# mLSTM cell and gated MLP on one core: the second chunk's queries change their queue, and their block transposes their place

## The chip, the cores and the metric

The kernel runs on one core of a Trainium2 chip. The metric is the device time of one execution in microseconds (us); a lower one is better. Times are given as the median of several runs. One execution was also profiled, and the views of the profile that are quoted here all come from it; their times count from the start of its span. The engines are PE (TensorE, with PEld its weight loads), DVE (VectorE), ACT (ScalarE), POOL (GpSimd) and SP (SyncE, which here only issues transfers). A name with q behind it, such as SPq, is the engine's sequencer, which issues transfers and waits.

## The reference

Two blocks follow each other. The first is an mLSTM cell over 768 time steps for 4 batches of 8 heads of 40 elements; the second is a dense layer, a quick GELU and another dense layer over the 3072 tokens.

```python
for t in range(S):                                   # S = 768
    m_new = np.maximum(f_gate[:, :, t] + m, i_gate[:, :, t])
    f_stab, i_stab = np.exp(f_gate[:, :, t] + m - m_new), np.exp(i_gate[:, :, t] - m_new)
    C = f_stab * C + i_stab * outer(v_t, k_t)        # 40 x 40 for each batch and head
    n = f_stab * n + i_stab * k_t
    y[:, :, t] = sigmoid(o_gate_t) * (C @ q_t) / max(|n . q_t|, 1)
x = y as (3072 tokens, 320)
h = x @ w_in                                         # 320 x 2048
out = (h * sigmoid(1.702 * h)) @ w_out               # 2048 x 320
```

## The kernel before

Time is cut into six chunks of 128 steps (`w` = 0 to 5), and the recurrence within a chunk becomes products of matrices: scores of keys and queries (`scores`, tile `p_s`), weighted by exponentials of the gates (`weights`, tile `wt`), times the values (`values`, tiles `p_o` and `p_i`), with a state that is carried from chunk to chunk (`carry`, tile `p_c`, which multiplies the keys by the values scaled by the gates, `vw`, and whose result DVE adds to the state in L611 and L579). For each chunk, the outputs of four batches are transposed into `xT` (512 tokens), go through the first product (`up` for chunk 0, `up_fast` later; tile `p_h`, then the GELU, L641) and the second product (`down`, later `down_fast`; tile `p_out`).

The order of all work is written out by hand: the program is issued in the order of the Python calls, each engine runs its own instructions in that order, and waits are put in where one instruction needs another's result. The main loop runs over the chunks. In chunk `w` the first product is cut into eight steps `j`, and between them stands what prepares chunk `w + 1`: loads, gates, transposes. The second product is cut into blocks `i`, and a table (`attention`) says after which block each part of the next chunk's cell runs. For chunk 0 the second product has 16 blocks of four 128 x 320 products; `carry` of chunk 1 comes after block 3, `scores` after block 6, `values` after blocks 8 and 9.

The weights come into the kernel as pairs of 32-bit words and are turned into fp32 on the chip. There are 20 pieces of 128 x 512; pieces 0 to 9 belong to `w_in` and pieces 10 to 19 to `w_out`. `fetch(n)` loads a piece through the sync queue (L167). `convert(n)` takes two ScalarE instructions (L243 and L247) and then four DVE instructions (L256, L257, L259, L265). These conversions run during the first product of chunk 0 (pieces 3 to 16) and in the second (17 before block 0, 18 before block 4, 19 before block 5).

For chunk 1 the queries are loaded by `load_squares` into the tile `q_sq`, by four transfers of 320 KB (L108). One quarter of the rows is written by each, so a reader needs all four. `block_transposes(1, n)` with n = 1, 3, 5, 7 then makes the transposed queries `qT` of batch n // 2, one DVE instruction each (L394), which `scores` and `values` read. The keys of chunk 1 are loaded by L120 and transposed on PE (`transposes`, L386, with ScalarE's copies L388).

In the sync queue the transfers of chunk 0's first product stand in this order: the keys of chunk 1 (L120, `t_sb`), pieces 10 to 12, the values of chunk 1 (L120, `v_st`), pieces 13 to 17, `spread` (L403: four transfers that spread the rows of the running maxima, `m_row`, over the partitions of `wt`), pieces 18 and 19, the output gates (L122, `eo`), and the gates of chunk 2 (L92). POOL issues the queries of chunk 1 behind `scale(0, 1)` (L588), and later the small rows of the gates (L304 to L352). After the transposes, `q_sq` serves as a buffer for the turned outputs (`seam_in`) and then takes the queries of chunk 2.

PSUM has two pools: `ps_m` with four tiles (`p_h`, `p_out` and others) and `ps_a` with two (`p_t`, `p_c`, `p_s`, `p_o`, `p_i`), so a product can only begin when a reader has freed the tile of an earlier one.

Of the kernel before, what the change touches and what calls it, by code (L numbers as in the profile page):

```python
# [26 lines left out]
def kernel(  # L27
# [12 lines left out]
    nc = tc.nc  # L40
    B, H, S, D = q.shape
    BH = B * H
# [27 lines left out]
    V, A, G, T = nc.vector, nc.scalar, nc.gpsimd, nc.tensor  # L70
# [28 lines left out]

        return k_of(w)[t, h, :] if w < 2 else k_st[t, h * D:h * D + DP]  # L100

    def load_squares(w, what, queue=nc.sync):
        for dst, src in [((k_sq, k), (q_sq, q))["kq".index(c)] for c in what]:
            x = src[:, :, w * L:(w + 1) * L, :].rearrange("b (p two) (r c) d -> two r (b p) (c d)", two=2, c=4)
            for i in range(2):
                for n in range(2):
                    r, at = slice(i * 64 + n * 32, i * 64 + n * 32 + 32), (1 - n) * 32
                    queue.dma_start(out=dst[r, at:at + BH // 2 * 4 * D].rearrange("r (j x) -> r j x", x=4 * D), in_=x[i])  # L108

    def load(w, what, bs=slice(0, B)):  # L110
        hs = slice(bs.start * H, bs.stop * H)
# [121 lines left out]
    def convert(n):  # L233
        convert_begin(n)
        convert_end(n)

    def convert_begin(n):
        convert_high(n)
        convert_low(n)
# [9 lines left out]
    def convert_end(n):  # L249
        convert_mid(n)  # L250
        convert_add(n)
# [88 lines left out]
    def masks():  # L340
        V.tensor_reduce(out=odd, in_=full.rearrange("p (j two) -> p two j", two=2)[:, 1], axis=AX.X, op=OP.add)
        V.memset(odd[BH:2 * BH, :], 0.0)
        V.tensor_scalar(out=even, in0=odd, scalar1=-1.0, scalar2=1.0, op0=OP.mult, op1=OP.add)
# [46 lines left out]
    def block_transposes(w, n):  # L390
        b, (to, name, src) = n // 2, ((kT, "kT", k_sq), (qT, "qT", q_sq))[n % 2]
        at, n = 32 + b * NP * 4 * D, NP * 4 * D
        to[w, b] = work.tile([128, NP, L], FP, tag=name, bufs=4, name=name)
        V.transpose(out=to[w, b].rearrange("d j (r c) -> d j c r", c=4),  # L394
                    in_=src[:, at:at + n].rearrange("r (j c d) -> r j c d", c=4, d=D)[:, :, :, 0:32])

    def spread(w):

        for c in range(2):
            x = wt[w, c] = work.tile([L, NJ, 2, HL], FP, tag="wt", bufs=2, name="wt")  # L400
            for n in range(2):
                src = m_row[w][n, c * PH:(c + 1) * PH].rearrange("h t -> (h t)")
                nc.sync.dma_start(out=x[n * HL:(n + 1) * HL].rearrange("s j i t -> s (j i t)"),  # L403
                                  in_=src.unsqueeze(0).to_broadcast([HL, PH * HL]))
# [177 lines left out]
    def scale(w, c, part=0, parts=1):  # L582
        n = PH // parts
        hs = slice(c * PH + part * n, c * PH + (part + 1) * n)
        if part == 0:
            vw[w, c] = work.tile([L, PH, D1], FP, tag="u", name="vw")
        e = cols[w][:, 2 * BH + hs.start:2 * BH + hs.stop].unsqueeze(2).to_broadcast([L, n, D1])
        G.tensor_tensor(out=vw[w, c][:, part * n:(part + 1) * n], in0=v_st[:, hs, :], in1=e, op=OP.mult)  # L588

    def wait_for(x):  # L590

        G.tensor_copy(out=mark, in_=x[:, 0:1])
# [21 lines left out]
    def up(w, j, between):  # L614


        x = xT[w].rearrange("p c b t -> p c (b t)")
        ph = {}

        def full(j, first, cs=range(2)):  # L620
            for c in cs:
                for i in range(2):
                    f = 2 * j + i
                    for n in range(2):
                        t = slice(n * W // 2, (n + 1) * W // 2)
                        T.matmul(ph[j][i][:, t], w_in_sb[:, c, f * 128:(f + 1) * 128], x[:, c, t],  # L626
                                 start=(first and c == 0 and n == 0), stop=(not first and c == 1 and n == 1))

        def rest(j, start, stop):
            n = 2 if j >= NF // 4 else 1  # L630
            for h in range(n):
                t = slice(h * W // n, (h + 1) * W // n)
                for i in range(2):
                    r = slice(i * 64, i * 64 + 64)
                    T.matmul(ph[j][i][:, t], w_in_x[r, j, :], x[r, 2, t], start=(start and h == 0),  # L635
                             stop=(stop and h == n - 1))

        def gelu(j):
            g = gs[w, j] = gp.tile([128, 2, W], FP, tag="g", name="g")
            for i in range(2):  # L640
                A.activation(out=g[:, i, :], in_=ph[j][i], func=AF.Gelu_apprx_sigmoid)  # L641

        def open_pair(j):
            ph[j] = [ps_m.tile([128, W], FP, tag="m", name="p_h") for _ in range(2)]

        open_pair(j)
        full(j, True, range(1 if j == 0 else 2))
        if j == 0:
            open_pair(1)
            full(1, True, range(1))  # L650
            full(0, True, range(1, 2))
        rest(j, False, True)
        gelu(j)
        between()
        if j:
            open_pair(j + 1)
        rest(j + 1, j > 0, False)
        full(j + 1, False, range(1 if j == 0 else 0, 2))
        gelu(j + 1)
# [178 lines left out]
    def run(calls):  # L838
        for f, *args in calls:
            f(*args)  # L840
# [62 lines left out]
    for w in range(NW):  # L903
        more = w + 1 < NW
        if w == 0:
            for j in range(NF // 2):
                if j % 2 == 0:
                    ahead, behind = converted[j // 2]
                    run([(convert, p) for p in ahead] + [(fetch, p) for p in fetched.get(j // 2, ())])
                    up(w, j, lambda: run([(columns_turn, 1) if p is None else (convert, p) for p in behind]))  # L910
                if j == 6:
                    load(1, "o")
                if j == 1:
                    wait_for(w_in_sb[:, 1, 512:1024])
                    scale(0, 1)
                    load_squares(1, "q", G)
                    load(1, "v")
                if j < B and j % 2:
                    carry(0, j // 2)
                if j == 3:  # L920
                    masks()
                    gates(1)
                    columns_in(1)
                if j == 4:
                    spread(1)
                if j >= B:
                    transposes(1, j - B)
                if j in (4, 5):
                    block_transposes(1, 2 * j - 7)
        else:  # L930
            token_sums(w)
            if more:
                gates(w + 1)
                load(w + 1, "o")
            for j in range(NF // 2):
                up_fast(w, j)
                if w == 1 and j < 4:
                    weight_sums(j)
                if more and j == 2:
                    load(w + 1, "vk")  # L940
                    columns_in(w + 1)
                    spread(w + 1)
                if more and j:
                    for n in ((), (0, 2), (4,), (6, 1), (3,), (5, 7), ())[j - 1]:
                        block_transposes(w + 1, n)
                if more and j == 7:
                    columns_turn(w + 1)
                if 2 <= j < 6:
                    hidden_difference(w, j - 2)
                if j >= 6:  # L950
                    hidden_sums(w, (j - 6,), G)
            gelu_fast(w, NF // 2 - 1)
            hidden_sums(w, (2, 3), V)
        side = attention(w + 1) if more else {}
        if w == 0:
            block_transposes(1, 5)
            block_transposes(1, 7)

            blocks = [(lambda b=b, n=n: down(w, b, n)) for n0 in (0, 2) for b in range(B) for n in (n0, n0 + 1)]
        else:  # L960
            blocks = down_fast(w, 0) + down_fast(w, 1)
        for i, block in enumerate(blocks):
            if w == 0 and i in (0, 4, 5):
                convert((17, 18, 19)[max(i - 3, 0)])
            if w + 2 < NW and i == (6 if w == 0 else 0):
                load_gates(w + 2)
            if w + 2 < NW and i == 13:
                load_squares(w + 2, "kq" if w else "k")
            if w == 0 and i == 15:
                load_squares(w + 2, "q")  # L970
            block()
            run(side.get(i, []))
            if w == 0 and i in (11, 13):
                input_sums(slice(0, 4) if i == 11 else slice(4, 8))
# [30 lines left out]
```

## Time and profile before

| what | value |
| --- | --- |
| median of 3 runs | 468.26 us (466.65 to 468.61) |
| the profiled execution, its own time | 469.14 us |
| its span | 467.4 us |
| PE busy | 460.4 us (99%) |
| DVE, ACT, POOL busy | 341.7, 189.6, 165.2 us |
| first product of chunk 0, last step to second product's first block | PE idle until 67.71 us |
| second product of chunk 0 | 67.71 to 112.6 us |
| L108 for chunk 1's queries, issued by POOL | 36.93 to 39.70 us |
| L394 for chunk 1's queries | two from 62.36 us, two from 76.21 us |

A line of a timeline has the start, the time from the first start to the last end, the engine, the line of the kernel, the operation, the tile written and the tiles read, and how many instructions of the kind stand together; in brackets is the idle time before it with what ended it. A line of the chain of waits has the start, the length and what ran. In the DMA view a queue's line has packets, megabytes and the time that its packets took as a share of the 16 transfer engines: q1 is the sync queue's, q10 ScalarE's, q0 the one for transfers issued by POOL. Ends of PE's instructions are modelled, so differences of starts are used for PE.

### The profile page before, as it was taken

Reading aid. Unit: us, or ns where it says so; the run is one execution under the profiler, and the core shown is the slowest. Engines: PE = TensorE matmul, PEld = TensorE weight load, DVE = VectorE, ACT = ScalarE, POOL = GpSimd, SP = SyncE. Lnnn points to the kernel's source line nnn. Section 1 sums busy time; section 2 is a strip of 40 time slices with the busy share of each in tenths; the row PEclk is TensorE's granted clock in tenths of the full one; section 3 lists DMA queues with packets and bytes.
Section 4 is the critical chain, followed back from the end, with each engine's and each line's share of the span. In section 5 each row is a group of like instructions: output and inputs, shape, how many; then the busy total and the mean of one; then the engine's idle time right before and its main releaser. Section 6 shows DMA issues by size and latency. Waiting matters only on the chain.

```text
span 467.4 us, 12367 instructions
## 1 busy us (share of the span) xinstructions
PE 460.4 (99%) x5063; PEld 387.4 (83%) x5063; DVE 341.7 (73%) x698; ACT 189.6 (41%) x433; POOL 165.2 (35%) x157
## 2 busy tenths in 40 slices
PE   8999999999999999999999999999999999999997
PEld 6867876776778999678999778999878999876996
DVE  5788779989788976688875778877768866545612
ACT  5686369500536700554800453900444810254100
POOL 5103314300798700266800257610148510157100
PEclk9999999999999999999999999999999999999999
DMA  8999999028995034988124999114999405000000
GB/s 164 194 275 191 193 270 234 6 61 185 172 147 119 3 80 128 193 120 134 34 60 113 199 131 162 22 41 117 182 133 120 94 18 139 28 1 0 1 29 29
DMA packets 133833, 52.87 MB, mean 113 GB/s; under 512 B 101984, under 2 KB 129584, under 8 KB 133776
## 3 DMA queue, kind: packets, MB, share of 16 engines
q1 hardware_dynamic: 125024, 48.96, 54.3%
q0 software_dynamic: 704, 1.46, 2.0%
q10 hardware_dynamic: 8048, 1.66, 1.8%
q8 instruction: 40, 0.66, 0.6%
q14 instruction: 17, 0.14, 0.1%
HBM read 44.52 MB, written 7.54 MB: 111 GB/s over the span
## 4 chain that ended last, share of the span: by engine, by line
PE 92%; ACT 2%; POOL 1%; DMA 1%; issue 1%; SPq 1%; DVE 1%; POOLq 0%; ACTq 0%; DVEq 0%
PE p_out L818 33%; PE p_h L709 27%; PE p_h L717 8%; PE p_out L764 6%; PE p_h L626 5%; PE p_c L602 2%; PE p_o L503 2%; PE p_s L459 2%; PE p_i L511 2%; PE p_h L635 1%; DMA bits<-in_moe_w_out_dram 1%; PE p_t L386 1%; PE p_s L448 1%; SPq L120 1%; ACT w_out_sb L243 0%
## 5 line engine op out<-in xcount | busy, mean ns | idle before, releaser
L755 POOL TENSOR_TENSOR g<-g,parts 128x512 f32<-128x512 f32 x30 | 38.2, 1273 | 188.5 <-DVE parts L747 181.1
L743 ACT COPY parts<-p_h 128x256 f32<-128x256 f32 x40 | 14.9, 374 | 149.4 <-PE p_h L709 147.5
L818 PE MATMUL p_out<-w_out_sb,g 128*128 128x160 f32 x480 | 69.5, 301 | 0.0
L818 PEld LDWEIGHTS p_out<-w_out_sb,g 128*128 128x128 f32 x480 | 66.5, 190 | 0.9
L709 PE MATMUL p_h<-xT,w_in_sb 128*128 128x256 f32 x240 | 67.0, 388 | 0.0
L690 ACT ACTIVATE g<-g 128x512 f32<-128x512 f32 x80 | 50.1, 631 | 39.2 <-DVE g L750 24.6
L709 PEld LDWEIGHTS p_h<-xT,w_in_sb 128*128 128x128 f32 x240 | 43.8, 190 | 18.5 <-issue 6.7
L823 DVE TENSOR_TENSOR o_sb<-o_sb,p_out 128x160 f32<-128x160 f32 x70 | 21.4, 317 | 41.2 <-PE p_out L818 40.6
L818 PE MATMUL p_out<-t_sb,s 128*128 128x160 f32 x320 | 47.2, 300 | 0.0
L746 DVE TENSOR_TENSOR t_x<-p_h,parts 128x256 f32<-128x256 f32 x40 | 16.6, 415 | 39.0 <-PE p_h L717 34.5
L818 PEld LDWEIGHTS p_out<-t_sb,s 128*128 128x128 f32 x320 | 44.4, 190 | 0.2
L709 PE MATMUL p_h<-t_x,s_in 128*128 128x256 f32 x160 | 41.1, 379 | 0.0
L717 PE MATMUL p_h<-xT,w_in_x 64*128 64x512 f32 (+1 forms) x192 | 39.8, 540 | 0.0
L435 ACT ACTIVATE wt<-wt,cols 128x64 f32<-128x64 f32 x160 | 38.8, 333 | 0.1
L764 PE MATMUL p_out<-w_out_sb,g 128*128 128x320 f32 x128 | 36.1, 437 | 1.0 <-ACT g L641 0.7
L709 PEld LDWEIGHTS p_h<-t_x,s_in 128*128 128x128 f32 x160 | 30.4, 190 | 4.2
L764 PEld LDWEIGHTS p_out<-w_out_sb,g 128*128 128x128 f32 x128 | 23.9, 190 | 11.1 <-ACT g L641 0.9
L747 DVE TENSOR_TENSOR parts<-p_h,t_x 128x512 f32<-128x512 f32 x40 | 27.7, 692 | 3.6
L754 ACT COPY g<-p_h 128x512 f32<-128x512 f32 x30 | 17.4, 580 | 30.4 <-PE p_h L717 25.1
L626 PE MATMUL p_h<-xT,w_in_sb 128*128 128x256 f32 x128 | 29.7, 385 | 0.0
L717 PEld LDWEIGHTS p_h<-xT,w_in_x 64*128 64x128 f32 x192 | 16.9, 186 | 14.7 <-issue 13.5
L750 DVE TENSOR_TENSOR g<-p_h,parts 128x512 f32<-128x512 f32 x40 | 27.6, 691 | 1.4
(204 smaller groups left out, 842.7 us busy)
## 6 DMA issues: line engine op xcount, KB each, us to landing
wt<-m_row SPq DMA_DIRECT2D x20, 256.0 KB, 5.0
k_sq<-in_k_dram SPq DMA_DIRECT2D x16, 320.0 KB, 6.4
q_sq<-in_q_dram SPq DMA_DIRECT2D x16, 320.0 KB, 10.4
out_dram<-o_sb SPq DMA_DIRECT2D x24, 160.0 KB, 1.9
eo<-in_o_gate_dram SPq DMA_DIRECT2D x5, 640.0 KB, 8.4
bits<-in_moe_w_in_dram SPq DMA_DIRECT2D x6, 512.0 KB, 10.9
q_sq<-x_row SPq DMA_DIRECT2D x10, 256.0 KB, 2.9
v_st<-in_v_dram SPq DMA_DIRECT2D x14, 160.0 KB, 5.0
```

Of the source, the lines that this page charges most:

```text
L435: A.activation(out=x[:, h, :], in_=x[:, h, :], func=AF.Exp, scale=-1.0, bias=cols[w][:, c * PH + h:c * PH + h + 1])
L626: T.matmul(ph[j][i][:, t], w_in_sb[:, c, f * 128:(f + 1) * 128], x[:, c, t], start=(first and c == 0 and n == 0), stop=(not first and c == ...
L690: A.activation(out=gs[w, j][:, i, :], in_=gs[w, j][:, i, :], func=AF.Gelu_apprx_sigmoid)
L709: T.matmul(out, a, x[n], start=start, stop=stop)
L717: T.matmul(row[:, t], w_in_x[r, j, :], rest_x[r, 2, t], start=(not late and h == 0), stop=(late and h == n - 1))
L747: V.tensor_tensor(out=y[:, half_w:3 * half_w].rearrange("p (a t) -> p a t", a=2), in0=flat[:, half_w:3 * half_w].rearrange("p (a t) -> p a ...
L750: V.tensor_tensor(out=g[:, 1, :], in0=row1, in1=y[:, half_w:3 * half_w], op=OP.add)
L754: A.copy(out=g[:, 0, :], in_=row0)
L755: G.tensor_tensor(out=g0, in0=g0, in1=u, op=OP.add)
L764: T.matmul(po, gs[w, f // 2][:, f % 2, b * L:(b + 1) * L], w_out_sb[:, f, :], start=(f == 0), stop=(f == NF - 1))
L818: T.matmul(po, a(f), b[:, f, :], start=(f == 0), stop=(f == NH - 1))
L823: V.tensor_tensor(out=dst, in0=x, in1=po, op=OP.add)
```

## The change

The four loads of chunk 1's queries go from POOL, where they stood behind `scale(0, 1)` in step j = 1, to the sync queue, behind `spread(1)` in step j = 4. The parameter `queue` of `load_squares` goes. The four block transposes of the queries, of which two stood in steps j = 4 and 5 and two ahead of the conversion of piece 17, now stand together behind that conversion, at the beginning of block 0 of the second product. Nothing else moves: the instructions of PE and ScalarE are the same in the same order, DVE and POOL and SP differ in these places alone.

```diff
-    def load_squares(w, what, queue=nc.sync):
+    def load_squares(w, what):
...
-                    queue.dma_start(out=dst[r, at:at + BH // 2 * 4 * D].rearrange("r (j x) -> r j x", x=4 * D), in_=x[i])
+                    nc.sync.dma_start(out=dst[r, at:at + BH // 2 * 4 * D].rearrange("r (j x) -> r j x", x=4 * D), in_=x[i])
...
                 if j == 1:
                     wait_for(w_in_sb[:, 1, 512:1024])
                     scale(0, 1)
-                    load_squares(1, "q", G)
                     load(1, "v")
...
                 if j == 4:
                     spread(1)
+                    load_squares(1, "q")
                 if j >= B:
                     transposes(1, j - B)
-                if j in (4, 5):
-                    block_transposes(1, 2 * j - 7)
...
         if w == 0:
-            block_transposes(1, 5)
-            block_transposes(1, 7)
 
             blocks = [(lambda b=b, n=n: down(w, b, n)) for n0 in (0, 2) for b in range(B) for n in (n0, n0 + 1)]
...
             if w == 0 and i in (0, 4, 5):
                 convert((17, 18, 19)[max(i - 3, 0)])
+                if i == 0:
+                    for n in (1, 3, 5, 7):
+                        block_transposes(1, n)
```

## The prediction

> **What bounds the kernel now.** I read the page first, then the chain of waits and the timelines of the stretch that the change touches (about 27 to 115 us), then the DMA view of parts of it. Two lines of the page:
>
> ```profile
> PE 460.4 (99%) x5063; PEld 387.4 (83%) x5063; DVE 341.7 (73%) x698; ACT 189.6 (41%) x433; POOL 165.2 (35%) x157
> DMA  8999999028995034988124999114999405000000
> ```
>
> TensorE is busy for all but 7.0 us of 467.4, so an edit that moves no matmul can only win back waits of PE, or add some. The DMA row has 9s in slices 1 to 6, which are 11.7 us each: from 12 to 82 us the transfer engines are full, and there the order of transfers decides what comes late. The chain of waits leaves PE in one long stretch near the change (start, length, what):
>
> ```profile
> 57.12 2.33 SPq L120
> ...
> 60.67 5.14 DMA bits<-in_moe_w_out_dram
> ...
> 76.35 0.52 POOL vw L588
> ...
> 80.08 6.66 PE p_out L764 x24
> ```
>
> It runs through the sync queue (v's load, L120), the landing of an output weight piece, ScalarE's conversions and POOL's `vw`, back to PE. PE's timeline has the stalls:
>
> ```profile
> 49.85 2.00 PE L635 MATMUL p_h<-xT,w_in_x 64*128 64x256 f32 x16
> 55.34 1.04 PE L386 MATMUL p_t<-ident,t_sb 128*128 128x128 f32 x8
> 56.29 3.72 PE L626 MATMUL p_h<-xT,w_in_sb 128*128 128x256 f32 x16
> 59.94 2.54 PE L635 MATMUL p_h<-xT,w_in_x 64*128 64x256 f32 x16
> 65.97 1.04 PE L386 MATMUL p_t<-ident,t_sb 128*128 128x128 f32 x8
> 67.71 3.50 PE L764 MATMUL p_out<-w_out_sb,g 128*128 128x320 f32 x12 [0.71 <-ACT g L641]
> 71.49 5.65 PE L764 MATMUL p_out<-w_out_sb,g 128*128 128x320 f32 x20 [0.28 <-DVE w_out_sb L265]
> 77.69 2.40 PE L602 MATMUL p_c<-vw,t_sb 64*64 64x41 f32 x128 [0.55 <-POOL vw L588]
> ```
>
> From start to start, so that modelled ends play no part: (a) the 16 L635 take 2.47 us (59.94 to the next group at 62.41) where the same 16 took 1.93 at 49.85: 0.54 lost. (b) Eight L386 to the next group: 1.74 here, 0.95 at 55.34: 0.79. (c) Twelve L764 take 3.78; 48 of them later run from 99.56 to 112.58, 0.271 each, so 3.35 with 0.1 for the first: 0.43. (d) Twenty take 6.20 against 5.42 and two changes of kind at 0.1: 0.58. (e) The 128 L602 take 2.32 to 80.01; the same 128 take 2.01 at 154.40: 0.31. Together 2.65 us, say 2.7, of the 7.0 that PE idles. All five stand behind ScalarE, which runs in order, and ScalarE stands behind DMA:
>
> ```profile
> 54.50 0.67 ACT L243 ACTIVATE w_out_sb<-s_in 128x512 f32<-128x512 f32 x1 [6.61 <-DMA s_in<-in_moe_w_out_dram]
> 65.91 0.69 ACT L243 ACTIVATE w_out_sb<-bits 128x512 f32<-128x512 f32 x1 [3.66 <-DMA bits<-in_moe_w_out_dram]
> ```
>
> A conversion waits for its piece, and the GELUs that free PE's banks (L641) and the exponentials that `vw` needs wait behind it.
>
> **The change, part by part.** *POOL's four issues go.* They are 2.77 us on POOL (36.93 to 39.70); its next work is at 49.04 and waits for DVE, so the issues themselves are worth 0. What they set off is not. The DMA view of 39 to 48 us:
>
> ```profile
> q0 software_dynamic: 358, 1.23, 81.4%
> q1 hardware_dynamic: 1630, 0.26, 28.9%
> ```
>
> The second chunk's queries (4 x 320 KB, 1.31 MB), issued by POOL, take four fifths of all engines for 9 us while the sync queue, with k and output pieces 10 to 12 queued, moves 0.26 MB. It moved 2.52 MB in the 7 us from 63. So POOL's load passes the sync queue and holds it up. How long? From above: k's last part is issued at 38.83 and lands at 53.23, the SP timeline's next step (v, 53.31) starts on that; k and v are of one size, and v's landings (60.60 to 63.19, issue 53.31) say some 10 us from first issue, so k, issued from 30.73 behind w_in pieces landing to 39.25, could be done near 43: 10 us. From below: 1.31 MB at the 196 GB/s that the windows show for 35 to 45 us is 6.7. Between them, 0.814 x 9 plus 0.6 for the edges is 7.9. I take 8, nearest to the measured engine time, and keep 6.7 to 10.
>
> [...]
>
> With 8 us less ahead of them, the pieces land when ScalarE is ready or before: piece 10 at 54.42-8 = 46.4 (ScalarE ends its last conversion at 47.89), piece 13 at 57.8 (ScalarE would reach it about 58). Then the GELUs follow PE, not DMA: that of tile 5 after full(5) at 55.5 instead of 60.24, that of tile 6 at 61 instead of 67.06, and (a), (b) go. Conversions 13 to 16 (four of 2.35 on DVE) then end near 70, not 76.2: (c) goes. ScalarE reaches the exponentials after GELU 7 (about 65.5 to 66.6), two kT copies 1.1, conversion 17 1.3 and the table load 1.28, about 71; `vw` (2 x 1.28) ends at 73.6, PE wants it at 77.69-2.4 = 75.3: (d), (e) go. What is late next is PE itself. Gain 2.7.
>
> *The four loads behind `spread` in the sync queue.* They now follow the last `wt` load and stand ahead of pieces 18 and 19, o and the gates. The sync timeline shows that each load starts when the one eight before has landed (L403 at 67.24, the landing at 67.16), so q's four start on the landings of pieces 15 to 17, 8 us earlier than 69.75 to 72.55: no delay there. `wt` last lands at 77.07-8 = 69.1. The price of q on this queue is read from the third chunk's: eight loads of the same shape land from 115.17 to 126.89, 1.67 each, 6.7 for four. Landing: 75.8 (73.8 to 77.1 by the bounds). Behind them pieces 18 and 19 (79.75 before), o (82.95) and gates lose 6.7 and gain 8: about 1 us earlier, and their users (ScalarE 84.31; DVE after 97) come later than that. Cost 0.
>
> *The block transposes.* At 62.36 two lay in idle time of DVE; two stood before conversion 17. Now all four stand behind it, ahead of the state updates:
>
> ```profile
> 76.21 2.07 DVE L394 STREAM_TRANSPOSE qT<-q_sq 128x512 f32<-128x512 f32 x2
> ...
> 82.65 0.49 DVE L611 TENSOR_TENSOR state_mid<-p_c,state_mid 128x328 f32<-128x328 f32 x1
> ...
> 91.53 2.35 DVE L462 TENSOR_TENSOR wt<-p_s,wt 128x1024 f32<-128x1024 f32 x2
> ```
>
> This adds a wait: DVE is in order, so behind the first transpose (which needs all four loads) stand the updates of L611 and L579 (which free p_c's banks for PE's p_s), conversions 18 and 19 and the products of L462, on which PE's p_o waits. Backwards from PE, now 2.7 earlier: p_o starts at 90.5 instead of 93.20; the first L462 (1.17) must start by 89.3; conversions 18 and 19 take 5.12 (86.41 to 91.53): 84.2; the updates 3.76 (82.65 to 86.41): 80.4; four transposes at 1.03: 76.3. Conversion 17 follows 16 at about 70 and, stretched beside POOL's work as it is now (4.5 us), ends by 74.5. So q may land as late as 76.3; 75.8 is expected, and 0.5 is the whole cover. If it is gone, each us of lateness costs one. At the bound 77.1, 0.8 of the gain is lost.
>
> **Sum.** The profiled execution took 469.14 (span 467.4 and 1.7 around it); with 2.7 less it is 466.4. It lies 0.88 above the median of the three runs (468.26), so the forecast for a median is 465.6. About 0.5%, 2.3 us, is what a measurement of this kernel can tell from no change; the gain is just beyond that. After L462 the order is unchanged and moves as a block.
>
> **Rivals.** *Late queries, part of the gain.* q lands between 76.3 and 79; PE gets its 2.7 and gives back up to all of it at p_s and p_o: 465.6 to 468.3. For it: the cover is 0.5 us. Against: k and v as above suggest 10 us of relief, a cover of 2.5.
>
> *The stalls have another owner.* Only (a) to (c), which hang on landings directly, go: 1.76, so 466.5; `vw` stays late behind ScalarE's own 11 us of conversions, GELUs, copies and table load. Against: ScalarE idles 6.61 and 3.66 us there now.
>
> *Slower: DVE waits on the queries.* Its place is the first block transpose. If the sync queue gains nothing from the absent POOL load (it may be held by its own 160-byte packets: k's and v's issues take 2.3 to 5.6 us each), q lands at 77.07+6.7 = 83.8. PE, not moved ahead, can bear 76.3+2.7 = 79.0, so p_o comes 4.8 later: 473.1. It decides from a landing of 81.3 on (2.3 us lost). For it: q moves from 51.45, its landing now, to a point where the queue is full. Against: the 81.4% row.
>
> *The change does nothing* in time: that needs the relief and the lateness to be equal; it is the middle of the first rival.
>
> **How the numbers follow.** Full gain 0.50 (465.6, 464.3 to 465.9); part of it, by the first two rivals, 0.35 (466 to 468.5); DVE waiting, slower, 0.15 (470.6 to 473). Faster by over 0.5% 0.50, within 0.35, slower 0.15. The range reaches from 464.3 (noise below the full gain) to 469.6, over both partial cases; it leaves out most of the slower one and a little below.
>
> **What would show it.** Right: no DMA wait of ScalarE before L243 between 47 and 62 us; L635 and L386 steps of 1.93 and 0.95; p_c from about 75.3; the L394 group as four in a row, starting near 76, with L611 behind it at about 80, and p_o near 90.5. The first broken step is a landing of q past 76.3: an idle time of DVE before L394 of more than 2 us, then PE waits at p_s or p_o. It is wrong if ScalarE still waits for pieces 10 and 13, or if p_o comes after 93.2.

## The result and the profile after

Over 20 runs each the changed kernel takes 466.48 us (466.00 to 467.16) and the kernel before 468.25 us (466.27 to 473.88); the ratio is 0.9954, with a 95% interval of 0.9935 to 0.9974. That is 0.46% less, 2.1 us by the ratio and 1.8 by the medians, just inside the 0.5% that the prediction counted as no change, though the interval does not reach 1. The lowest times differ by only 0.3 us; the highest by 6.7. The profiled execution took 466.95 us, its span 465.2.

Two lines of the page of the changed kernel, PE's busy time and the DMA row:

```profile
PE 459.8 (99%) x5063; PEld 387.8 (83%) x5063; DVE 340.3 (73%) x698; ACT 189.5 (41%) x433; POOL 163.5 (35%) x153
DMA  8999998049993045996034988024999306000000
```

Transfers fill the engines as before until slice 6. What changed is their order. (Landings of single transfers, here and below, are the trace's own records of them; no line of a view prints each.) The DMA view of the same 39 to 48 us in which POOL's load held four fifths of the engines:

```profile
q1 hardware_dynamic: 4244, 2.08, 104.6%
```

The sync queue now moves 2.08 MB there instead of 0.26. k's last part lands at 44.00 instead of 53.23, and the last part of piece 16 at 60.02 instead of 70.01. ScalarE waits for no transfer between 44 and 80 us; in its waits there, PE is what it waits for (line of the kernel and releaser, us in all, times, the longest):

```profile
ACT g L641 <- PE p_h L635: 4.7, 2, 2.7
```

PE's timeline of the changed kernel: the groups that lost time before, with full(5), the L626 group before the first of the two L386 groups, ahead of them, and p_s (L459) and p_o (L503) behind:

```profile
52.26 3.72 PE L626 MATMUL p_h<-xT,w_in_sb 128*128 128x256 f32 x16
...
60.24 2.00 PE L635 MATMUL p_h<-xT,w_in_x 64*128 64x256 f32 x16
62.17 3.72 PE L626 MATMUL p_h<-xT,w_in_sb 128*128 128x256 f32 x16
65.73 1.04 PE L386 MATMUL p_t<-ident,t_sb 128*128 128x128 f32 x8
66.60 8.78 PE L764 MATMUL p_out<-w_out_sb,g 128*128 128x320 f32 x32
75.31 2.08 PE L602 MATMUL p_c<-vw,t_sb 64*64 64x41 f32 x128
...
83.97 2.09 PE L459 MATMUL p_s<-qT,kT 40*64 40x64 f32 x128
...
90.50 1.14 PE L503 MATMUL p_o<-v_st,wt 64*64 64x41 f32 x64
```

The steps from start to start are 1.93 for L635 (2.47 before), 0.87 for L386 (1.74), 8.71 for the 32 products of L764 in one piece (9.98 in two) and 2.01 for L602 (2.32). No bracket stands behind any of them. The kernel before has at these places:

```profile
51.78 3.72 PE L626 MATMUL p_h<-xT,w_in_sb 128*128 128x256 f32 x16
...
86.67 2.10 PE L459 MATMUL p_s<-qT,kT 40*64 40x64 f32 x128
...
93.20 1.14 PE L503 MATMUL p_o<-v_st,wt 64*64 64x41 f32 x64
```

From full(5) to p_s it is 31.71 us in the changed kernel, against 34.89 before: 3.18 us of stalls are gone. DVE's timeline of the changed kernel:

```profile
75.13 4.03 DVE L394 STREAM_TRANSPOSE qT<-q_sq 128x512 f32<-128x512 f32 x4
78.94 0.56 DVE L611 TENSOR_TENSOR state_mid<-p_c,state_mid 128x328 f32<-128x328 f32 x1
...
86.92 2.35 DVE L462 TENSOR_TENSOR wt<-p_s,wt 128x1024 f32<-128x1024 f32 x2
92.65 0.84 DVE L517 TENSOR_TENSOR u<-p_i,cols 128x656 f32<-128x656 f32 x1 [3.38 <-PE p_i L511]
```

The four transposes follow conversion 17 without a wait. The queries landed at 73.27, 1.9 us ahead, and L462 is done so early that DVE then idles 3.38 us for PE.

The span is 2.2 us shorter, not 3.2. The starts of equal instructions in the two traces differ by +0.5 us already after the first 6 us of the kernel, where nothing was changed, and another 0.45 is lost later, 0.25 at 149 us and 0.2 behind PE's last product. In the other executions below, full(5) begins between 0.4 us earlier and 1.0 later than in the first execution of the kernel before, so the first part is the difference of two executions and not the change. What costs the other 0.45 is open.

### The profile page after: what moved, and what is told of

It reads as the page before. It is cut to its first block, busy times and chain, and to the rows that moved or that the text cites. A ratio compares the mean times of both kernels' runs of the same rounds, so it can differ in the third digit from the quotient of the medians.

```text
span 465.2 us, 12360 instructions
## 1 busy us (share of the span) xinstructions
PE 459.8 (99%) x5063; PEld 387.8 (83%) x5063; DVE 340.3 (73%) x698; ACT 189.5 (41%) x433; POOL 163.5 (35%) x153
## 4 chain that ended last, share of the span: by engine, by line
PE 88%; POOL 4%; DMA 3%; DVE 2%; issue 1%; ACT 0%; SPq 0%; DVEq 0%; POOLq 0%
PE p_out L818 33%; PE p_h L709 21%; PE p_h L717 7%; PE p_h L626 6%; PE p_out L764 6%; PE p_c L602 3%; DMA q_sq<-in_q_dram 2%; PE p_o L503 2%; PE p_s L459 2%; PE p_i L511 2%; PE p_h L635 2%; PE p_t L386 1%; POOL g L755 1%; PE p_s L448 1%; POOL g L786 1%
## 5 line engine op out<-in xcount | busy, mean ns | idle before, releaser
L764 PE MATMUL p_out<-w_out_sb,g 128*128 128x320 f32 x128 | 35.7, 436 | 0.0
L764 PEld LDWEIGHTS p_out<-w_out_sb,g 128*128 128x128 f32 x128 | 23.9, 190 | 9.6
L626 PE MATMUL p_h<-xT,w_in_sb 128*128 128x256 f32 x128 | 29.6, 384 | 0.0
```

What stands on the lines that cost most here:

```text
L764: T.matmul(po, gs[w, f // 2][:, f % 2, b * L:(b + 1) * L], w_out_sb[:, f, :], start=(f == 0), stop=(f == NF - 1))
```

## The experiments

Six kernels change one thing each; one of them was profiled twice, and the kernel before five times more. Times are medians, and a ratio is to the kernel before, which was timed anew beside them (468.81 us for the first four kernels, 467.96 for the next two).

**The loads alone.** `load_squares(1, "q")` moves behind `spread(1)`, the block transposes stay where they were.

```diff
-                    load_squares(1, "q", G)
...
                     spread(1)
+                    load_squares(1, "q")
```

> The four loads go to the sync queue behind the maxima's rows; the block transposes stay where they were (steps 4 and 5, and two ahead of conversion 17). Theory (the loads free the sync queue, but their landing near 73 us needs the transposes late): DVE reaches the first transpose at about 61.5 us and waits until the queries land at 73.3, with conversions 13 to 16 behind it; block 1 of the second product can begin at about 80 instead of 68.6, and p_o comes near 100: some 10 us later than in the changed kernel, 7 later than before, about 475 us. Rival (the transposes' place is free, only the loads matter): 466.5, as the changed kernel.

Measured: 478.66 us, ratio 1.0203 (1.0142 to 1.0265). A line of DVE's timeline and one of PE's:

```profile
73.99 1.99 DVE L394 STREAM_TRANSPOSE qT<-q_sq 128x512 f32<-128x512 f32 x2 [13.53 <-DMA q_sq<-in_q_dram]
```
```profile
78.30 9.72 PE L764 MATMUL p_out<-w_out_sb,g 128*128 128x320 f32 x24 [9.77 <-DVE w_out_sb L265]
```

DVE waits 13.5 us for the queries, and PE for the conversions behind them. The place of the wait is that of the theory, and its size within 2 us (61.5 to 73.3 expected, 60.5 to 74.0 measured). The time is 3.7 us over its figure, and the second line says where most of that is: 24 products take 9.72 us instead of 6.6. PE's granted clock is 0.50 in every window from 74 to 84 us, that is, in the end of its wait and in the first 5.9 us of these products, which loses 2.9 us. The late place of the transposes is a condition of the late loads.

**The transposes alone.** The loads stay on POOL in step 1, the four transposes stand behind conversion 17 as in the changed kernel.

```diff
-                if j in (4, 5):
-                    block_transposes(1, 2 * j - 7)
...
-            block_transposes(1, 5)
-            block_transposes(1, 7)
...
                 convert((17, 18, 19)[max(i - 3, 0)])
+                if i == 0:
+                    for n in (1, 3, 5, 7):
+                        block_transposes(1, n)
```

> The loads stay on POOL in step 1; the four block transposes stand together behind conversion 17. Theory (all of the gain is from the loads): PE's stalls between 60 and 80 us stay, conversion 17 begins 2.1 us earlier and the four transposes end at about 84.8 instead of 82.7, so L611 and then L462 are 2.1 later and p_o waits up to 1.6 us: 468 to 470, not faster than before. Rival (the gain is from DVE's order): about 466.5.

Measured: 468.68 us, ratio 0.9997 (0.9967 to 1.0027), as the theory had it. Two of PE's waits in the profiled execution:

```profile
PE p_c L602 <- POOL vw L588: 1.0, 2, 0.7
PE p_out L764 <- ACT g L641: 0.5, 1, 0.5
```

PE needs 34.31 us from full(5) to p_s, 2.60 more than in the changed kernel. Four of the five stalls are there (only the L635 have their 1.93), so DVE's order is not the gain.

**Early in the sync queue.** The transposes as in the changed kernel; the loads in step 1, but issued by SP.

```diff
-                    load_squares(1, "q", G)
+                    load_squares(1, "q")
```

> The loads go to the sync queue but stay in step 1, ahead of v and pieces 13 to 17; the transposes stand as in the changed kernel. If the place is what pays (q goes behind what is urgent): pieces 10 to 12 land as early as in the changed kernel, v and pieces 13 to 17 some 6.5 us later, the conversion of 13 waits until about 64, and the stalls after GELU 6 come back in part: 467 to 468. If the issuer is what pays (POOL's transfers hold up the sync queue's more than their bytes are worth): 466.5 as the changed kernel, since all of POOL's share is gone.

Measured: 467.59 us (466.54 to 472.87), ratio 0.9987 (0.9951 to 1.0022): the median is where the first theory had it, but the times spread as widely as those of the kernel before, and the profiled execution (466.54) has no stall of PE at all, 31.71 us from full(5) to p_s. Its ScalarE waited all the same:

```profile
61.07 0.66 ACT L243 ACTIVATE w_out_sb<-bits 128x512 f32<-128x512 f32 x1 [3.85 <-DMA bits<-in_moe_w_out_dram]
```

A second profiled execution of the same kernel took 473.35 us:

> The kernel with the loads early in the sync queue, unchanged, once more: its times lie between 466.5 and 472.9. Theory: here v and pieces 13 to 17 have little cover, so in a longer execution ScalarE's wait for piece 13 (3.9 us in the profiled one) is longer and PE stalls again at p_out or p_c; in a short one PE has no stall. Rival: the longer ones have no stall there and lose elsewhere.

There ScalarE's wait for piece 13 is 6.81 us, the last part of piece 16 lands at 69.98 instead of 66.32, and PE waits 1.88 us for `vw`, which the first execution did not; its clock is halved behind that (0.50 in the windows from 80 to 86 us). So q ahead of v and pieces 13 to 17 can just be borne or not at all, whichever queue issues it.

**Late on POOL.** The transposes as in the changed kernel; the loads stay with POOL but stand behind the gates' rows.

```diff
-                    load_squares(1, "q", G)
...
                     columns_in(1)
+                    load_squares(1, "q", G)
```

> The loads stay on POOL but are issued behind the gates' rows (about 60 us instead of 37); the transposes stand as in the changed kernel. If the place is what pays: k, v and pieces 10 to 16 land as in the changed kernel, PE's five stalls are gone, and 466 to 467 follows; the rows for wt may land some 5 us later (72 instead of 67), which costs the exponentials up to 2 us of a cover of 2.4. If the issuer is what pays: POOL's load takes most of the engines again, now ahead of pieces 17 to 19 and the wt rows, and half or more of the gain is lost: 467.5 to 469.

Measured: 466.25 us (465.66 to 466.66), ratio 0.9946 (0.9920 to 0.9973), the same as the changed kernel within the intervals, and as narrow. The DMA view of 61 to 70 us:

```profile
q0 software_dynamic: 433, 1.05, 61.5%
q1 hardware_dynamic: 369, 0.87, 42.7%
```

POOL's load again takes most of the engines, now behind pieces 13 to 17 and beside the `wt` rows; `q_sq` is complete at 73.94 and PE has no wait between 55 and 96 us. The place pays, not the issuer.

**No load.** The kernel before, without the four loads of chunk 1's queries.

```diff
-                    load_squares(1, "q", G)
```

> The kernel before without the four loads of chunk 1's queries (q_sq keeps chunk 0's, so chunk 1's results are of the wrong queries); everything else stays. Theory (POOL's load holds up the sync queue and is the cause of the five stalls): the stalls are gone, 465.5 to 466.5, like the changed kernel, and the times lie as close together as those of the changed kernel (about 1 us from lowest to highest). Rival (the transfer's own bytes do not matter, the sync queue is held by its 160-byte packets): 467.5 to 469, stalls and spread of times as before.

Measured: 466.36 us (466.00 to 466.85), ratio 0.9962 (0.9934 to 0.9990); 31.71 us from full(5) to p_s. All five stalls are gone. Removing the transfer is worth no more than moving it, so in its new place it costs nothing that these intervals can tell.

**Later still.** The changed kernel with the loads in step 6 instead of 4, behind pieces 18 and 19 and the output gates.

```diff
                     load(1, "o")
+                    load_squares(1, "q")
...
-                    load_squares(1, "q")
```

> The changed kernel with the four loads one step later still: behind pieces 18 and 19 and the output gates in the sync queue. They land at about 79.4 to 80.5 us instead of 73.3, and DVE, which reaches the first transpose at 75.1, waits 4.3 to 5.4 us. Theory (the cover between the landing and PE's need is about 4 us, of which 1.9 lie ahead of the transposes): p_o, which needs L462, is 1.9 to 3.0 late, and the time is that of the changed kernel plus as much: 468.4 to 469.5. Rival (DVE's later idle time takes all of it): 466.5, as the changed kernel.

Measured: 472.40 us (471.18 to 474.24), ratio 1.0093 (1.0064 to 1.0122), 5.9 us over the changed kernel where 1.9 to 3.0 were expected. A line of DVE's timeline, then three of PE's:

```profile
80.29 3.90 DVE L394 STREAM_TRANSPOSE qT<-q_sq 128x512 f32<-128x512 f32 x4 [5.79 <-DMA q_sq<-in_q_dram]
```
```profile
85.81 3.46 PE L459 MATMUL p_s<-qT,kT 40*64 40x64 f32 x128 [2.37 <-DVE state L611]
89.20 6.65 PE L764 MATMUL p_out<-w_out_sb,g 128*128 128x320 f32 x16
95.78 1.14 PE L503 MATMUL p_o<-v_st,wt 64*64 64x41 f32 x64
```

The landing (80.16), DVE's wait and PE's wait of 2.37 us are as worked out. But then PE needs 9.97 us from p_s to p_o, where the changed kernel takes 6.53. The windows view of two microseconds there (window, its length, busy time of PE, PEld, DVE, ACT and POOL with their instructions, granted clock of PE, DMA share, GB/s):

```profile
88.00:90.00 2.00, 2.00 (x50) 1.69 (x45) 1.83 (x4) 0.00 (x0) 0.00 (x0) 0.50 0.03 8
```

PE's clock is halved behind its own wait: 2.44 us of waiting (34.15 from full(5) to p_s, less 31.71) and 3.44 of half speed make the 5.9. The theory had the wait and not the clock.

**The kernel before, five executions more.**

> The kernel before, unchanged, profiled once more: its timed executions lie between 466.3 and 473.9 us. If the sync queue's lag behind POOL's load is what differs, the span differs from 467.4 by as much as the five stalls together differ from 2.7 us, and the landing of k's last part (53.23) moves with them. If the spread is from elsewhere, the stalls are 2.7 again and the difference lies outside 59 to 80 us.

> As the run before this one, once more: two executions more of the kernel before, to see whether a fast and a slow one differ in the stalls between 59 and 80 us or elsewhere.

> The kernel before, unchanged, once more, to meet one of its longer executions (470 us and over). Theory: the sync queue's lag behind POOL's load differs from execution to execution, and where it makes PE wait for over 2 us at one place the granted clock falls to 0.5 for some us, as it did behind the 2.37 us wait of the kernel with the later loads: a span of 468.5 and over shows a longer stall between 55 and 80 us, k's last landing past 53.2, or both, and a window with a clock of 0.5. Rival: the stalls are as in the other executions and the longer span comes from the first 30 us or the tail.

> As the run before this one: another execution of the kernel before, with the same theory and rival. The sum of PE's five stalls should follow the landing of k's last part.

> As the two runs before this one: another execution of the kernel before, with the same theory and rival. The sum of PE's five stalls should follow the landing of k's last part.

They took 467.14, 467.34, 467.69, 473.31 and 467.89 us. This table has them with the first profiled execution, in the order of the landing of piece 16's last part; the stall is the time from full(5) to p_s less 31.71.

| time, us | k's last part lands | piece 16 lands | stall, us |
| --- | --- | --- | --- |
| 467.14 | 49.06 | 68.02 | 1.42 |
| 467.34 | 50.04 | 68.23 | 1.60 |
| 467.69 | 49.81 | 68.55 | 2.06 |
| 467.89 | 50.48 | 68.91 | 2.25 |
| 469.14 (the first) | 53.23 | 70.01 | 3.18 |
| 473.31 | 46.77 | 71.20 | 7.72 |

So the stalls differ from execution to execution, and they order the times. They go with the landing of piece 16, ScalarE's last conversion before GELU 7, not with that of k as I expected: the longest execution has the earliest k. Piece 16 is not always what ScalarE waits for: in four of the six it waits for it (0.45 to 2.04 us); in the other two, the first and 467.89, its last wait is for piece 13 (3.66 and 6.28), and it goes through 14 to 16 without one.

The five places of the first execution are not those of all: in the three shortest PE loses time only at p_c, and L635 and L386 have the steps of the changed kernel. A line of the shortest:

```profile
75.51 1.14 PE L602 MATMUL p_c<-vw,t_sb 64*64 64x41 f32 x64 [0.85 <-POOL vw L588]
```

The longest has this wait and this clock, from PE's timeline and the windows view:

```profile
78.65 1.40 PE L602 MATMUL p_c<-vw,t_sb 64*64 64x41 f32 x64 [3.14 <-POOL vw L588]
80.35 1.95 PE L602 MATMUL p_c<-vw,t_sb 64*64 64x41 f32 x64 [0.30 <-POOL vw L588]
```
```profile
76.00:78.00 2.00, 0.00 (x0) 0.00 (x0) 1.93 (x4) 1.95 (x6) 0.68 (x1) 1.00 1.04 306
82.00:84.00 2.00, 2.00 (x16) 1.33 (x13) 1.85 (x4) 2.00 (x10) 1.93 (x3) 0.50 0.15 34
```

Behind the wait of 3.14 us for `vw` the clock is halved from 79.4 to 86.2 us, by windows of one microsecond: 6.8 us, so 3.4 lost. That is why 1.2 us more lag in piece 16 than in the first execution cost 4.5 us more. The mean granted clock of every timed execution says that this is no single case. Of the 50 executions of the kernel before beside these experiments, 38 have 0.999 or 1.000 and take 465.71 to 470.64 us, and 12 have 0.992 to 0.996 and take 469.84 to 473.33; the 20 of the changed kernel have 0.998 or more. What makes the lag differ between executions of one program is open.

## Why the prediction was right or wrong

**The mechanism was right.** POOL's early load held up the sync queue (0.26 MB from 39 to 48 us, against 2.08 with the load late); ScalarE stood behind the pieces, PE behind ScalarE. With the load gone or late (no load, late on POOL, the changed kernel) PE's five stalls are zero; with only the transposes moved four of them stay. In the changed kernel p_c came at 75.31 (75.3 was worked out) and p_o at 90.50 (90.5). That these agree so closely is luck: counted from full(5) the relief was 2.86 us at p_c and 3.18 at p_o, not 2.4 and 2.7, and the profiled execution was 0.48 us behind at full(5).

**The relief was under-sized and harmless.** I took 8 us out of 6.7 to 10; k gained 9.2 and piece 16 gained 10.0, the upper bound, which was the one made from k's and v's own landings. That too is against one execution: against the other five k gained 2.8 to 6.5 and piece 16 8.0 to 11.2. The queries landed at 73.27 (75.8, at the earliest 73.8), so the cover that I put at 0.5 us was larger: DVE came to the transposes at 75.13 with 1.9 us in hand. The updates took 3.28 us (3.76) and conversions 18 and 19 4.70 (5.12). POOL's L439 ended at 81.30, within the updates, where before it ran to 86.96, beside nearly all of them and the start of conversion 18; that this is why they were shorter is not shown. L462 began at 86.92, where 89.3 would have done. The rival of the late queries, a landing between 76.3 and 79, was not met.

**The term that was mis-sized is the sum of the stalls.** In the execution that I read they were 3.18 us, not 2.65: my normal steps still had 0.1 us at each change of kind and 0.95 for L386, where the undisturbed kernel shows 0.87 and no such steps, and the L386 and L626 groups ahead of (a) had lost 0.08 and 0.10 that I did not count. That is the small part. The larger is that this one execution, 0.88 us above the median of its kernel, was taken for all of them: I subtracted its stall from the median as well. Four of the six executions in the table have 1.4 to 2.3 us of stall, the median of the six is 2.2, and the gain by the ratio is 2.1. The profiled execution was forecast at 466.4 and took 466.95; the median was forecast at 465.6 and is 466.48.

**The chances** gave 0.50 to a gain of over 0.5% and 0.35 to less; the measured 0.46% falls in the second, not by either of its two mechanisms, but because the full gain is smaller in a typical execution. So the time lies in the stated range only because the range reached over the partial cases; the full gain's own range, 464.3 to 465.9, lies below all 20 times. That the kernel before also has executions near 473, and the changed one none in 20, was not forecast.

**The rival on the slower side** (the sync queue gains nothing, 473.1) did not occur. The kernel with later loads shows its place: DVE at the first transpose, landing at 80.16. The point from which it decides was wrong: I gave 1 us for each us of lateness and named 81.3, but with the halved clock a landing 1.1 us ahead of that already made the kernel 0.9% slower than before.

**The issuer.** Late on POOL (466.25 us, ratio 0.9920 to 0.9973) and late on SP (466.48, 0.9935 to 0.9974) differ by nothing that these intervals can tell. It does not follow that an early load on another queue is free: with the one on POOL the median is 468.25.

## What to carry to other kernels

Where transfers fill the engines, as here, a load that is issued from another queue before it is needed can go past the queue with the urgent ones (1.23 MB beside their 0.26, from 39 to 48 us), and its price then stands at the consumers of those, several engines away. Move it to where its landing just precedes its use, and move its consumers in an in-order engine with it; here either half alone gained nothing or lost 2%. When a stall is read from one execution, profile a few more before its size is taken off a median: here it ran from 1.4 to 7.7 us.

## What the hardware showed

In three traces PE's granted clock fell to 0.50 within 1.6 us after a wait of 1.88 us (early in the sync queue, the second execution, where a second wait of 0.56 had begun), 2.37 us (later still) and 3.14 us (before, 473.31), for 6.8 us each time by windows of one microsecond; it did not fall after one of 1.49 us (before, 467.69). This made a stall of 2.4 us cost 5.9. Mean clocks of 0.996 in executions without a trace are about half that loss: an estimate from 0.4% of 470 us is 1.9 us lost, or 3.8 us at half speed.

The queue that POOL issues into moved 1.23 MB in 358 packets, 3.4 KB each, beside 1630 packets of the sync queue with 0.26 MB, 160 bytes each (39 to 48 us, before). Large packets beside small ones left the sync queue 0.03 MB in a microsecond; how the engines share themselves between the queues was not tried further.
